# Batch 0 of a fused attention, gated-MLP and GLU kernel in another order, with its high parts on ScalarE, and w_out2's loads put behind batch 3's last weight piece

## The chip, the cores and the metric

One core of one Trainium2 chip runs the whole program. The metric is device time in microseconds (us). One run's profiled execution gives the trace; the times of other runs have no profile.

Five engines run their own instruction streams and wait for each other through semaphores: TensorE (PE, with its weight loads as PEld), VectorE (DVE), ScalarE (ACT), GpSimd (POOL) and SyncE (SP), which here only starts DMA transfers. Each engine works in order: an instruction that waits holds back everything behind it on its engine.

## The reference, cut to what matters

```python
# q, k, v: (4 batches, 8 heads, 576, 64)
scores = q @ k.T / 8 - slope[h] * |i - j|, kept where 0 <= i - j < 128
attn   = softmax(scores)
x      = concat_heads(attn @ v)                      # (4, 576, 512)
h      = gelu_tanh(x @ w_in)                         # w_in (512, 1024)
u, v   = h[..., :512], h[..., 512:]
vn     = (v - mean(v)) / sqrt(var(v) + 1e-6) * g_ln
vs     = w_sg @ vn + b_sg                            # mixes the 576 positions
x2     = x + (u * vs) @ w_out                        # (4, 576, 512)
h2     = relu(x2 @ w_in2)                            # w_in2 (512, 1024)
conv   = three-tap convolution of h2 over positions, per channel
out    = (h2 * sigmoid(conv)) @ w_out2               # w_out2 (1024, 512)
```

All inputs lie in DRAM; w_in, w_out, w_in2, w_out2 and the convolution's taps are 64-bit floats, read as pairs of 32-bit words.

## The kernel before, in words

**Precision.** Each large matrix product is made of three products of 32-bit "r" tiles: high by high, high by low, low by high. So each operand needs a high part (`copy` into a rounded tile, L188) and a low part (`tt`, the operand minus its high part, L200). `split` (L217) makes both. A 64-bit weight is first narrowed to 32 bits (`narrowed`, L268): a magnitude (L279 on ACT or L281 on DVE), a clamp (L283) and three bit operations on DVE (L284 to L286). The dictionary `ON` names which engines may take each kind of high and low part; `pick` (L177) takes the one with the least booked time.

**Phases.** STEPS holds three strings of steps, run in order. A step is a letter and indices. The first string is batch 0's attention in lower-case letters, then, woven together, batch b's MLP (capital V, U, G, W) and batch b+1's attention (capital L, M, C, E, N, T, A). The second is batch 3's MLP, the third the GLU (D and F). Names used below:

- `k` (L718) loads the position tables, the identity for transposes and g_ln, b_sg.
- `l m.half`, `v m.half` load q, k and v of head pair m (0 to 3); half 0 is rows 0 to 255, half 1 rows 256 to 575. The tag "st" has four buffers.
- `c` scores (PE `sc`, then masked by DVE into `t`, L530), `e` exponentials on ACT, `n` the division by the row sums (DVE `r`, then `scaled`, L215), `t` transposes (PE `pT`, evicted into `ph`), `z` the product with v (PE `o`, evicted into `x`).
- `X b.m.half` splits x into `xh`, `xl`.
- `j half.k` loads a piece of w_in, `i half.k` narrows and splits it into `win`. Half 1 is v's columns (four pieces, each one k-slice); half 0 is u's (four pieces, each one block m of 128 columns).
- `V b.j` (L608): v's product for rows block j (PE `psv`, 12 matmuls), gelu on ACT, mean and variance on DVE, then vn's high and low part. It needs all four pieces `i1.*`.
- `U b.half.m` (L638): u's product for column block m (PE `psu`, 12 matmuls), gelu. U0.0.m needs piece `i0.m`.
- `G` (PE `pss`, then L691 on DVE), `W` (PE `pso`, then x2 written to DRAM).
- `g` prepares w_sg (`prep32`), `o` w_out, `a i.c` a piece of w_in2 or w_out2: loaded, narrowed, split. Pieces prepared before the GLU's buffers exist are written to DRAM (`w2d`); the last twelve of w_in2 (LATE) go straight into their place.
- `w i.k.n` (L751) loads from DRAM what was prepared: w_in2's first part (i = 0, `w`) and w_out2 (i = 1, `wout`, eight transfers of 512 KB). Its instructions keep their place in the program.
- `x`, `y` load and split x2 for the GLU; D is the GLU's first product (PE `psg` from `x2g`), F its second (PE `psg` from `wout`).

A scheduler of the framework turns the list into one order for each engine by its own model of time; instructions under `keep_in_program_order` keep their place in the list. One tag "g" of two PSUM banks serves psv, psu, pss, pso in turn: a third product waits until the first is evicted.

The second string, where w_out2's loads stand:

```python
s = weave(n[:-6], put_by[LATE:]) + n[-6:]
for k in range(4):
    for h in range(2):
        s.insert(s.index("W3.0.0") + 3 * (2 * k + h), f"w1.{k}.{h}")
```

`n` is batch 3's MLP (29 steps), and `put_by[LATE:]` the last twelve pieces of w_in2.

## Time and profile before

| what | value |
|---|---|
| median of 3 runs | 599.72 us (599.45 to 600.98) |
| the profiled execution | 601.56 us, of which the trace's span is 599.8 us |
| granted TensorE clock, mean | 0.971 of full |
| busy PE / PEld | 561.9 / 483.6 us |
| busy DVE / ACT / POOL | 380.0 / 241.0 / 297.5 us |

Busy time counts instructions on an engine, not waiting. The chain of waits goes back from the last instruction to whatever released it; what an engine idles off that chain costs nothing. The profiled execution is 1.84 us above the median of the runs.

### The profile page before, as it was taken

Reading aid. Unit: us, or ns where it says so; the run is one execution under the profiler, and the core shown is the slowest. Engines: PE = TensorE matmul, PEld = TensorE weight load, DVE = VectorE, ACT = ScalarE, POOL = GpSimd, SP = SyncE. Lnnn points to the kernel's source line nnn. Section 1 sums busy time; section 2 is a strip of 40 time slices with the busy share of each in tenths; the row PEclk is TensorE's granted clock in tenths of the full one; section 3 lists DMA queues with packets and bytes.
Section 4 is the critical chain, followed back from the end, with each engine's and each line's share of the span. In section 5 each row is a group of like instructions: output and inputs, shape, how many; then the busy total and the mean of one; then the engine's idle time right before and its main releaser. Section 6 shows DMA issues by size and latency. Waiting matters only on the chain.

```text
span 599.8 us, 10377 instructions
## 1 busy us (share of the span) xinstructions
PE 561.9 (94%) x3744; PEld 483.6 (81%) x3744; DVE 380.0 (63%) x957; ACT 241.0 (40%) x610; POOL 297.5 (50%) x456
## 2 busy tenths in 40 slices
PE   6897499999999999999999899799799999999998
PEld 5564477879889798789798798799698889898887
DVE  4783658784485995795985787566865554545400
ACT  5484125863024743118732111244454434433401
POOL 2757512993142652344652543529877455545500
PEclk8896799899999999999999999899999999999999
DMA  8852014242225254241335335360210300100011
GB/s 283 280 186 81 23 40 146 87 130 62 84 75 146 60 166 148 87 145 37 119 104 158 105 107 152 130 209 1 74 43 19 114 19 19 55 19 19 17 54 53
DMA packets 44083, 57.78 MB, mean 96 GB/s; under 512 B 4096, under 2 KB 28672, under 8 KB 44032
## 3 DMA queue, kind: packets, MB, share of 16 engines
q1 hardware_dynamic: 43888, 56.99, 30.4%
q8 instruction: 29, 0.48, 0.3%
q14 instruction: 22, 0.18, 0.1%
q10 hardware_dynamic: 144, 0.13, 0.1%
HBM read 42.43 MB, written 14.68 MB: 95 GB/s over the span
## 4 chain that ended last, share of the span: by engine, by line
PE 64%; DVE 16%; POOL 8%; ACT 5%; DMA 3%; issue 2%; SPq 1%; POOLq 0%; ACTq 0%; DVEq 0%
PE psg L186 28%; PE psv L186 7%; PE pso L186 7%; PE psu L186 6%; PE sc L186 5%; PE o L186 5%; PE pss L186 3%; PE pT L446 2%; ACT t L160 2%; POOL t L215 2%; DVE wa L285 2%; DMA w<-in_w_in_dram 2%; DVE t L215 1%; DVE wa L283 1%; DVE wa L284 1%
## 5 line engine op out<-in xcount | busy, mean ns | idle before, releaser
L186 PE MATMUL psg<-x2g,w 128*128 128x288 f32 x768 | 108.0, 299 | 1.6 <-DVE x2g L204 1.2
L186 PEld LDWEIGHTS psg<-x2g,w 128*128 128x128 f32 x768 | 105.8, 191 | 3.9 <-DVE x2g L204 2.0
L186 PE MATMUL psg<-wout,gh 128*128 128x512 f32 (+1 forms) x272 | 81.3, 384 | 1.8 <-ACT gh L195 1.8
L160 ACT ACTIVATE t<-t,st 128x256 f32<-128x256 f32 (+2 forms) x144 | 67.2, 469 | 16.3 <-DVE st L530 9.9
L215 POOL TENSOR_SCALAR t<-t,r 128x256 f32<-128x256 f32 (+2 forms) x109 | 59.1, 558 | 19.5 <-DVE r L545 13.0
L186 PE MATMUL pss<-wsg,vn 128*128 128x256 f32 (+1 forms) x448 | 65.8, 304 | 2.7 <-DVE t L691 2.7
L186 PE MATMUL psu<-xh,win 128*128 128x256 f32 (+1 forms) x256 | 54.8, 308 | 11.1 <-POOL win L198 6.7
L186 PEld LDWEIGHTS pss<-wsg,vn 128*128 128x128 f32 x448 | 61.7, 195 | 4.1 <-DVE t L691 3.5
L817 DVE SCALAR_TENSOR_TENSOR cc<-hb,cw,cc 128x576 f32<-128x576 f32 x32 | 28.6, 893 | 50.0 <-POOL cc L215 50.0
L186 PE MATMUL pso<-gh,wo 128*128 128x256 f32 (+1 forms) x256 | 55.3, 308 | 5.0 <-DVE t L691 4.4
L186 PEld LDWEIGHTS psg<-wout,gh 128*128 128x128 f32 x272 | 49.5, 189 | 12.1 <-ACT gh L195 2.4
L186 PEld LDWEIGHTS psu<-xh,win 128*128 128x128 f32 x256 | 43.1, 198 | 13.6 <-POOL win L198 6.9
L186 PE MATMUL psv<-win,xh 128*128 128x512 f32 (+1 forms) x160 | 52.0, 403 | 1.8 <-POOL win L198 1.8
L186 PE MATMUL psg<-wout,gl 128*128 128x512 f32 (+1 forms) x136 | 52.2, 385 | 0.1
L215 POOL TENSOR_SCALAR cc<-hb,cw 128x576 f32<-128x576 f32 x32 | 27.6, 864 | 46.1 <-ACT hb L813 46.0
L186 PEld LDWEIGHTS pso<-gh,wo 128*128 128x128 f32 x256 | 41.1, 190 | 7.7 <-DVE t L691 4.8
L204 POOL TENSOR_TENSOR gl<-gg,gh 128x512 fp32r<-128x512 f32 x32 | 46.6, 1458 | 1.3 <-ACT gh L195 1.3
L204 POOL TENSOR_TENSOR t<-t,u 128x256 f32<-128x256 f32 (+1 forms) x32 | 27.7, 870 | 37.6 <-DVE t L691 28.9
L186 PE MATMUL sc<-k,q 64*128 64x256 f32 (+2 forms) x288 | 43.1, 372 | 0.2 <-DMA q<-in_q_dram 0.2
L813 ACT ACTIVATE hb<-psg 128x576 f32<-128x576 f32 x32 | 20.8, 652 | 55.7 <-PE psg L186 54.0
L186 PE MATMUL o<-ph,V 128*64 128x128 f32 (+2 forms) x448 | 41.1, 308 | 1.9 <-ACT ph L195 1.7
L204 DVE TENSOR_TENSOR gg<-cc,hb 128x576 f32<-128x576 f32 x32 | 30.3, 953 | 17.7 <-ACT cc L160 17.3
(87 smaller groups left out, 1069.9 us busy)
## 6 DMA issues: line engine op xcount, KB each, us to landing
w<-in_w_out_dram SPq DMA_DIRECT2D x24, 256.0 KB, 3.1
x2s<-x2d SPq DMA_DIRECT2D x16, 288.0 KB, 3.0
w<-in_w_in_dram SPq DMA_DIRECT2D x8, 512.0 KB, 5.6
w<-in_w_in_dram SPq DMA_DIRECT2D x16, 256.0 KB, 2.8
wout<-w2d SPq DMA_DIRECT2D x8, 512.0 KB, 4.4
V<-in_v_dram SPq DMA_DIRECT2D x12, 320.0 KB, 3.3
out_dram<-ot SPq DMA_DIRECT2D x15, 256.0 KB, 2.0
k<-in_k_dram SPq DMA_DIRECT2D x12, 288.0 KB, 3.2
```

What stands on the lines that cost most here:

```text
L160: ins = nc.scalar.activation(*args, **kw)
L186: return nc.tensor.matmul(out, lhsT, rhs, start=start, stop=stop, **kw)
L204: return (nc.vector if eng == "dve" else nc.gpsimd).tensor_tensor(dst, a, b, op=op)
L215: e.tensor_scalar(dst, src, col, 1.0, op0=ALU.mult, op1=ALU.mult)
L283: tc.keep_in_program_order(clamp.tensor_scalar(f(a), f(a), W_LOW, W_HIGH, op0=ALU.max, op1=ALU.min))
L284: nc.vector.tensor_scalar(a, a, 0x07FFFFFF, 3, op0=ALU.bitwise_and, op1=ALU.logical_shift_left)
L285: nc.vector.scalar_tensor_tensor(a, high, 0xC0000000, a, op0=ALU.bitwise_and, op1=ALU.bitwise_or)
L446: nc.tensor.transpose(ps[:, n * P : (n + 1) * P], s["t"][:, c0 : c0 + P], ident)
L813: nc.scalar.activation(h[:, 1 : S + 1].rearrange("p (a n) -> p a n", a=2), ps[:, :, :288], AF.Relu)
L817: nc.vector.scalar_tensor_tensor(cc, h[:, 0:S], cw[:, 0, c : c + 1], cc, op0=ALU.mult, op1=ALU.add)
```

## The change

In batch 0's list the steps stand in another order: V0.0 and V0.1 are parted, i0.2 stands before U0.0.0 and i0.3 before U0.0.2, and the second-half loads of pair 1 stand early, in buffers of another tag (w64). The tables are loaded per head pair in four transfers, not in two. The engines of batch 0's parts are fixed: the high parts of w_in, of x and of vn on ScalarE; the low parts of w_in and of x's first half on GpSimd; the divisions of the odd head (but for its last block) on VectorE and the others on GpSimd; the even head's evictions of first-half transposes on VectorE. The magnitude of six of w_in's eight pieces is on ScalarE. `prep32` (w_sg) keeps its high part's place in the list. In the second string w_out2's eight loads stand among the last six steps, behind the last piece of w_in2.

```diff
--- before.py
+++ after.py
@@ -35,9 +35,9 @@
 SLACK = 6000.0
 
 ON = {
-    "clamp": "dve", "w64 hi": "pool", "w64 lo": "pool", "w32 hi": "act pool", "w32 lo": "dve",
+    "clamp": "dve", "win hi": "act", "win lo": "pool", "w64 hi": "pool", "w64 lo": "pool", "w32 hi": "act pool", "w32 lo": "dve",
     "norm": "dve pool",
-    "x hi": "act pool", "x lo": "dve", "vn hi": "pool", "vn lo": "dve",
+    "x hi": "act pool", "x lo": "dve", "x first hi": "act", "x first lo": "pool", "x late hi": "act", "x late lo": "dve", "vn first hi": "act", "vn first lo": "dve", "vn hi": "pool", "vn lo": "dve",
     "gate": "pool", "g hi": "act dve pool", "g lo": "dve pool", "x2 hi": "act pool", "x2 lo": "dve",
     "tap": "act pool", "glu": "dve", "a hi": "act", "a lo": "pool",
     "edge hi": "pool", "edge lo": "pool",
@@ -73,10 +73,11 @@
     ]
     put_by = [f"a{i}.{c}" for i in (1, 0) for c in range(16)]
     s = """
-        k0 l0.0 k2 l1.0 k1 v0.0 l2.0 v1.0 l3.0 v2.0 v3.0 j1.0 j1.1 c0.0 e0.0 c1.0 n0.0 e1.0 i1.0 c2.0 e2.0 t0.0 n1.0 c3.0
-        e3.0 z0.0 X0.0.0 l0.1 v0.1 c0.1 e0.1 n2.0 t1.0 z1.0 X0.1.0 j1.2 j1.3 i1.1 n3.0 l1.1 v1.1 t2.0 z2.0 c1.1 e1.1 n0.1 i1.2
-        t3.0 z3.0 X0.2.0 X0.3.0 i1.3 j0.0 l2.1 c2.1 e2.1 n1.1 j0.1 t0.1 z0.1 j0.2 j0.3 i0.0 l3.1 v2.1 c3.1 e3.1 V0.0 V0.1 n2.1
-        t1.1 z1.1 i0.1 U0.0.0 X0.0.1 i0.2 n3.1 t2.1 v3.1 z2.1 X0.1.1 U0.0.1 i0.3 t3.1 z3.1 U0.0.2 U0.0.3 X0.2.1 X0.3.1 k3
+        k0 l0.0 k1 l1.0 k5 k2 l2.0 v0.0 k3 l3.0 v1.0 j1.0 v2.0 v3.0 j1.1 l1.1
+        c0.0 e0.0 c1.0 e1.0 l0.1 n0.0 j1.2 v0.1 c2.0 e2.0 t0.0 n1.0 c3.0 e3.0 l2.1 j1.3 v1.1 i1.0 z0.0 X0.0.0 t1.0 n2.0 z1.0 X0.1.0
+        i1.1 t2.0 n3.0 z2.0 X0.2.0 c0.1 e0.1 l3.1 j0.0 i1.2 t3.0 z3.0 X0.3.0 c1.1 e1.1 i1.3 n0.1 c2.1 e2.1 j0.1 j0.2 t0.1 n1.1 z0.1
+        v2.1 i0.0 c3.1 e3.1 j0.3 V0.0 t1.1 n2.1 z1.1 v3.1 i0.1 V0.1 t2.1 n3.1 z2.1 i0.2 U0.0.0 t3.1 z3.1 X0.0.1 U0.0.1
+        X0.1.1 i0.3 U0.0.2 X0.2.1 X0.3.1 U0.0.3 k4
     """.split()
     for b in range(B - 1):
         p = NP * (b + 1)
@@ -109,9 +110,8 @@
     n[n.index("W3.1.0")] += " y0.2"
     n[n.index("W3.1.1")] += " y0.3"
     s = weave(n[:-6], put_by[LATE:]) + n[-6:]
-    for k in range(4):
-        for h in range(2):
-            s.insert(s.index("W3.0.0") + 3 * (2 * k + h), f"w1.{k}.{h}")
+    late = [f"w1.{k}.{h}" for k in range(4) for h in range(2)]
+    s = s[:-6] + weave(s[-6:], late)
     second = " ".join(["x0.0.1.2.3"] + s)
     return first, second
 
@@ -265,7 +265,7 @@
 
     STAGE = dict(st=S, vn=1024, w64=512)
 
-    def narrowed(src, n, pool, tag, bufs, spool, stag, sbufs, act_abs=True):
+    def narrowed(src, n, pool, tag, bufs, spool, stag, sbufs, act_abs=False):
 
         if spool is None:
             st = src
@@ -275,7 +275,7 @@
         words = st[:, : 2 * n].rearrange("p (n w) -> p n w", w=2)
         low, high = words[:, :, 0], words[:, :, 1]
         a = pool.tile([P, 256 if tag == "wa" else 512], U32, tag=tag, name="wa", bufs=bufs)[:, :n]
-        if stag == "vn" and act_abs and pick(dict(act=52 + 0.85 * n, dve=67 + 0.52 * n)) == "act":
+        if act_abs:
             tc.keep_in_program_order(nc.scalar.activation(f(a), f(high), AF.Abs))
         else:
             tc.keep_in_program_order(nc.vector.tensor_scalar(a, high, 0x7FFFFFFF, None, op0=ALU.bitwise_and))
@@ -294,7 +294,8 @@
     def prep32(hi, lo, src, n, pool, tag, bufs):
         st = pool.tile([P, S], F32, tag=tag, name="wst", bufs=bufs)
         nc.sync.dma_start(st[:, :n], src)
-        split(hi, lo, st[:, :n], "w32")
+        tc.keep_in_program_order(copy(hi, st[:, :n], engines=ON["w32 hi"]))
+        tt(lo, st[:, :n], f(hi), ALU.subtract, ON["w32 lo"])
 
     def cols(w, k, c0, n):
 
@@ -311,12 +312,12 @@
             nc.sync.dma_start(st.rearrange("p (k n) -> p k n", k=NK), cols(w_in, slice(0, NK), k * P, P))
 
     def w_in_piece(half, k):
-        a = narrowed(w64.pop((half, k)), HF, mpool, "u", 4, None, "vn", 5, half == 1)
+        a = narrowed(w64.pop((half, k)), HF, mpool, "u", 4, None, "vn", 5, half == 1 or k < 2)
         if half:
-            split(winh[:, k, HF:], winl[:, k, HF:], a, "w64")
+            split(winh[:, k, HF:], winl[:, k, HF:], a, "win")
         else:
             sl = slice(k * P, (k + 1) * P)
-            split(winh[:, :, sl], winl[:, :, sl], a.rearrange("p (k n) -> p k n", k=NK), "w64")
+            split(winh[:, :, sl], winl[:, :, sl], a.rearrange("p (k n) -> p k n", k=NK), "win")
 
     def w_sg_piece(c):
         if c == 0:
@@ -479,14 +480,15 @@
         s = st8.setdefault((0, m), {})
         if half == 0:
             kq = apool.tile([P, 512], F32, tag="st", name="kq", bufs=NST)
-            s["k"], s["q"] = kq[:, :256], kq[:, 256:]
-            (nc.scalar if m == 0 else nc.sync).dma_start(s["q"], qT[0, m, :, :256])
-            nc.sync.dma_start(s["k"], kT[0, m, :, :256])
-        else:
-            s["k"] = apool.tile([P, 448], F32, tag="st", name="k", bufs=NST)
-            s["q"] = apool.tile([P, 320], F32, tag="st", name="q", bufs=NST)
-            nc.sync.dma_start(s["k"], kT[0, m, :, 128:])
-            nc.sync.dma_start(s["q"], qT[0, m, :, 256:])
+            s["k", half], s["q", half] = kq[:, :256], kq[:, 256:]
+            (nc.scalar if m == 0 else nc.sync).dma_start(s["q", half], qT[0, m, :, :256])
+            nc.sync.dma_start(s["k", half], kT[0, m, :, :256])
+        else:
+            tag, bufs = ("w64", 2) if m == 1 else ("st", NST)
+            s["k", half] = apool.tile([P, 448], F32, tag=tag, name="k", bufs=bufs)
+            s["q", half] = apool.tile([P, 320], F32, tag=tag, name="q", bufs=bufs)
+            nc.sync.dma_start(s["k", half], kT[0, m, :, 128:])
+            nc.sync.dma_start(s["q", half], qT[0, m, :, 256:])
 
     def z_vload(m, half):
         if half == 0:
@@ -521,7 +523,7 @@
             if of not in banks:
                 banks[of] = aps.tile([P, 512], F32, tag="a", name="sc", bufs=NA)
             d = slice(j * D, (j + 1) * D)
-            q, k = s["q"][d, q0 - 256 * half :][:, :nq], s["k"][d, k0 - 128 * half :][:, :nk]
+            q, k = s["q", half][d, q0 - 256 * half :][:, :nq], s["k", half][d, k0 - 128 * half :][:, :nk]
             mm(banks[of][d if i == 4 else slice(0, P), o : o + nk], q, k, start=True, stop=True)
         for j, i in z_blocks(half):
             o, nk = BLK[i][6], BLK[i][3]
@@ -546,7 +548,7 @@
         book("dve", 170)
         for j, i in z_blocks(half):
             e, c, _ = z_weights(m, half, j, i)
-            scaled(e, e, r[:, c - a : c - a + 1], ON["norm"])
+            scaled(e, e, r[:, c - a : c - a + 1], "dve" if j and i < 4 else "pool")
 
     def z_transpose(m, half):
         s = st8[0, m]
@@ -567,7 +569,7 @@
                 load["pe"] += 110
                 nc.tensor.transpose(ps[:, n * P : (n + 1) * P], src, ident)
             n = len(srcs) * P
-            copy(ph[:, :n], ps[:, :n], True)
+            copy(ph[:, :n], ps[:, :n], True, "act" if half or j else "dve")
             s["ph", half, j] = ph
 
     def z_av(m, half):
@@ -597,7 +599,7 @@
         x = xs[b, m][:, HALF[half]]
         hi = mpool.tile([P, n], F32R, tag=f"xg{half}", name="xh", bufs=8)
         lo = mpool.tile([P, n], F32R, tag=f"xg{half}", name="xl", bufs=8)
-        split(hi, lo, x, "x")
+        split(hi, lo, x, "x" if b else "x late" if half else "x first")
         xg[b, m, half] = (hi, lo)
 
 
@@ -632,7 +634,7 @@
         nc.gpsimd.tensor_scalar(rs[:r], ba[:r, 1:2], 1.0, 1e-6, op0=ALU.mult, op1=ALU.add)
         nc.gpsimd.tensor_tensor(rs[:r], rs[:r], mhalf[:r], op=ALU.pow)
         nc.vector.tensor_scalar(v[:r], v[:r], ba[:r, 0:1], rs[:r], op0=ALU.subtract, op1=ALU.mult)
-        split(hi[:r], lo if j < 4 else hi[64:], v[:r], "vn")
+        split(hi[:r], lo if j < 4 else hi[64:], v[:r], "vn" if b else "vn first")
         vns[b, j] = (hi, lo)
 
     def m_u(b, half, m):
@@ -716,11 +718,9 @@
 
 
     def constants(i):
-        if i == 0:
-            nc.sync.dma_start(tab[:, :1], tables[:, :1])
-        elif i == 1:
-            nc.sync.dma_start(tab[:, 1:], tables[:, 1:])
-        elif i == 2:
+        if i < NP:
+            nc.sync.dma_start(tab[:, i : i + 1], tables[:, i : i + 1])
+        elif i > NP:
             nc.sync.dma_start(ident, ident_c)
         else:
             nc.sync.dma_start(gln, g_ln)
```

## Rows read from the trace of the kernel before

**Rows 1.** Stages: window, length, each engine's busy us (instructions), granted clock, DMA

```profile
0.00:100.00 100.00, 80.89 (x511) 57.69 (x511) 61.92 (x208) 44.53 (x127) 48.52 (x80) 0.86 0.46 146
160.00:320.00 160.00, 158.59 (x1193) 135.46 (x1190) 126.15 (x407) 70.55 (x221) 73.37 (x130) 1.00 0.36 108
320.00:440.00 120.00, 109.37 (x708) 100.85 (x707) 85.38 (x156) 35.91 (x64) 64.17 (x90) 0.99 0.38 117
```

**Rows 2.** TensorE in order of time, 40 to 72 us (start, length, idle before)

```profile
50.90 1.22 PE L186 MATMUL psv<-win,xh 128*128 128x512 f32 x2 [0.33 <-POOL win L198]
...
69.87 0.58 PE L186 MATMUL psu<-xh,win 128*128 128x256 f32 x1 [6.72 <-POOL win L198]
```

**Rows 3.** GpSimd in order of time, 44 to 57 us

```profile
44.55 5.28 POOL L215 TENSOR_SCALAR t<-t,r 128x256 f32<-128x256 f32 x5 [0.85 <-DVE r L545]
49.81 1.04 POOL L198 TENSOR_SCALAR win<-wa 128x512 fp32r<-128x512 f32 x1
50.83 2.23 POOL L215 TENSOR_SCALAR t<-t,r 128x256 f32<-128x256 f32 x5
```

**Rows 4.** A slice of batch 0, columns as in the first group

```profile
50.00:60.00 10.00, 8.65 (x58) 5.70 (x58) 0.86 (x2) 4.41 (x9) 6.15 (x9) 0.69 0.23 64
```

**Rows 5.** VectorE in order of time, 50 to 71 us

```profile
57.82 0.49 DVE L204 TENSOR_TENSOR xl<-x,xh 128x320 fp32r<-128x320 f32 x1 [7.45 <-ACT xh L195]
...
69.38 0.98 DVE L286 SCALAR_TENSOR_TENSOR wa<-w,wa 128x512 uint32<-128x512 uint32 x1
```

**Rows 6.** psu's instructions alone, at the full and at the low clock

```profile
60.00:63.20 3.20, 3.13 (x24) 2.92 (x24) 0.39 (x1) 1.00 0.35 102
71.50:76.60 5.10, 5.07 (x23) 4.98 (x23) 0.38 (x1) 0.50 0.00 0
```

**Rows 7.** GpSimd's costliest groups, 0 to 77 us (busy us, mean ns, idle)

```profile
L215 POOL TENSOR_SCALAR t<-t,r 128x256 f32<-128x256 f32 x24 | 15.1, 642 | 3.9 <-ACT wa L279 1.9 <-DVE r L545 1.9
...
L198 POOL TENSOR_SCALAR win<-wa 128x512 fp32r<-128x512 f32 x8 | 6.2, 770 | 6.6 <-DVE wa L286 6.6
L215 POOL TENSOR_SCALAR t<-t,r 128x128 f32<-128x128 f32 x8 | 3.9, 492 | 11.1 <-DVE r L545 11.1
```

**Rows 8.** VectorE's divisions, one form, 160 to 240 us

```profile
L215 DVE TENSOR_SCALAR t<-t,r 128x256 f32<-128x256 f32 x12 | 5.3, 497 | 0.1
```

**Rows 9.** VectorE's groups, 0 to 77 us

```profile
L204 DVE TENSOR_TENSOR xl<-x,xh 128x256 fp32r<-128x256 f32 (+1 forms) x8 | 4.4, 547 | 8.8 <-ACT xh L195 7.5 <-POOL xh L198 1.4
...
L204 DVE TENSOR_TENSOR wsg<-wst,wsg 128x576 fp32r<-128x576 f32 x3 | 2.4, 806 | 0.0
L281 DVE TENSOR_SCALAR wa<-w 128x512 uint32<-128x512 uint32 x5 | 2.0, 404 | 0.9 <-DMA w<-in_w_in_dram 0.9
...
L197 DVE COPY ph<-pT 128x384 f32<-128x384 f32 x1 | 0.5, 545 | 0.0
```

**Rows 10.** ScalarE's groups, 0 to 77 us

```profile
L279 ACT ACTIVATE wa<-w 128x512 f32<-128x512 f32 x3 | 2.0, 683 | 0.0
...
L195 ACT CAST xh<-x 128x320 fp32r<-128x320 f32 x4 | 1.9, 466 | 0.0
```

**Rows 11.** Chain of waits, 374 to 384 us (start, us, what)

```profile
374.83 6.35 DMA w<-in_w_in_dram
```

**Rows 12.** VectorE in order of time, 376 to 383 us

```profile
381.20 0.29 DVE L281 TENSOR_SCALAR wa<-w 128x256 uint32<-128x256 uint32 x1 [4.24 <-DMA w<-in_w_in_dram]
```

**Rows 13.** TensorE in order of time, 378 to 385 us

```profile
383.13 0.56 PE L186 MATMUL pso<-gh,wo 128*128 128x320 f32 x2 [3.62 <-DVE t L691]
```

**Rows 14.** SyncE's issues, 372 to 377 us

```profile
372.97 0.32 SPq L761 DMA_DIRECT2D wout<-w2d  x1
```

**Rows 15.** Page, DMA issues: count, KB each, median us to landing

```profile
w<-in_w_in_dram SPq DMA_DIRECT2D x16, 256.0 KB, 2.8
```

**Rows 16.** psg's instructions alone, before and behind that wait

```profile
366.60:368.40 1.80, 1.74 (x12) 1.61 (x12) 0.00 (x0) 1.00 0.63 148
384.70:387.50 2.80, 2.73 (x12) 2.75 (x12) 0.00 (x0) 0.53 0.00 0
```

## The prediction

> **What bounds the kernel now.** I first read the table by stage. From 160 to 320 us TensorE is busy 158.6 of 160 us at the full clock; from 0 to 100 us only 80.9, at 0.86 of the clock, and from 320 to 440 us 109.4 of 120 [rows 1]. So time can be had at two places, which the change touches, and between them TensorE passes on a shift one for one.
>
> Then I read TensorE's order in batch 0. Its last psu columns wait 6.72 us, to 69.87 us, for GpSimd's high part of a w_in piece, and before that the fourth k-slice of psv starts at 50.90, as another high part ends [rows 2]. GpSimd's order shows why: from 44.55 us on it works without a pause, five divisions, a high part, five divisions, more parts [rows 3]. What should be seen: the first five divisions take 5.28 us and the next five 2.23 us. They are the same work; the second five ran while VectorE, 0.86 us busy in that slice, stood still [rows 4]. VectorE waits 7.45 us there, to 57.82, for `xh`, which hangs on those divisions through the transposes; its last step on a w_in piece ends only at 70.36 us [rows 5]. The price is paid again in the clock: 24 psu matmuls take 3.13 us at the full clock, and behind the wait 23 take 5.07 us at half of it [rows 6].
>
> **Batch 0, part by part.**
>
> *GpSimd.* It loses the divisions of j = 1 but for its last block (16: 12 by 642 ns and 4 by 492 ns, 9.7 us), eight high parts of win (6.2 us) [rows 7] and the four high parts of x's first half. It gains four low parts of 256 columns; the trace has no such x, and I bound one by a win high part above (770 ns) and by half of it below, 1.5 to 3.1 us. The trace's 9.7 and 6.2 less 1.5 to 3.1 make some 13 to 14 us less, in an engine that paces 44 to 57 us. In that stretch two of each five divisions go (5.28 by 2/5 is 2.11, 2.23 by 2/5 is 0.89), and two high parts, the one shown with 1.04 us and one at the mean of 0.77 (sum 1.81) [rows 3, 7]. That is 4.8 us earlier for psv's last slice, for the transposes behind the divisions and so for `xh`.
>
> *VectorE.* It gains those 16 divisions, at most 497 ns each, 8.0 us [rows 8], and three more evictions of 545 ns, 1.6 us. It loses four low parts of x (2.2 us), three magnitudes (1.2 us) and, since w_sg's high part keeps its place behind the batch, three w_sg low parts (2.4 us) [rows 9]. Net +3.8 us. What hides it: the 7.45 us for which it waited [rows 5]. Without that cover it costs 3.8 us, and I keep that for the range. The three w_sg pieces come back behind U0.0.3, with u's and v's later blocks queued behind them on ScalarE and VectorE and pss waiting for the last; VectorE is busy 61.9 of the first 100 us [rows 1], so I take 0, and 2.4 us if there is no room.
>
> *ScalarE.* It gains eight high parts of 512 columns and three magnitudes, which I price alike, by the magnitude of that width: 11 by 683 ns, 7.5 us; and four xh at no more than 466 ns, 1.9 us [rows 10]. It is 4.4 us busy in the ten from 50 to 60 us [rows 4], so half of it fits where it waited; the rest falls among the exponentials before 45 us. I take 0 on the path, with 9.4 us as the other end.
>
> *Order.* The piece i0.2 stands before U0.0.0 rather than behind X0.0.1, so its VectorE work can fill the 7.45 us; i0.3 stands no earlier against t3.1 than it did. I give this nothing beyond covering VectorE's 3.8 us. Where psu then doesn't stand still for 6.72 us, the clock holds: 24 matmuls at the rate of 5.07 us for 23 are 5.3 us, against 3.13, so 2.2 us come back [rows 6]. The tables in four transfers and pair 1's loads in w64 change arrivals by a few tenths of a microsecond; 0. The high parts of vn change engine at about the same price; 0.
>
> Sum for batch 0: 4.8 + 2.2 = 7.0 us. Low end: no gain and 9.4 us of ScalarE's work in series, so 9.4 lost. High end: the whole wait of 6.7 us besides, 13.7 gained.
>
> *A rule against the change.* The rows show that a division on GpSimd takes 1.06 us beside a full VectorE and 0.45 us beside an idle one [rows 3, 4]. The Trainium skill ("GPSIMD Engine Reference", section 8, Key points) says that GpSimd shares its SBUF interfaces with VectorE and contends with those of VectorE's instructions that run in a two-port mode or have two SBUF inputs. Read strictly, divisions split over both engines hardly run side by side, and only the high parts (1.8 us) would come off the 44 to 57 us stretch, not 4.8; the sum would be 3.0 us less, 591.2 us. No row has a division on both at once, so I keep the row's arithmetic and count this among the rivals.
>
> **w_out2's loads.** The chain of waits holds a 256 KB load of w_in2, issued at 374.83 us, for 6.35 us [rows 11]. VectorE stands 4.24 us before its first instruction on it [rows 12], and queued behind it is L691's eviction of pss, which frees the PSUM bank that pso needs: TensorE waits 3.62 us [rows 13]. A 512 KB load of w_out2 went out at 372.97 on the same queue [rows 14]. The median of such w_in2 loads is 2.8 us [rows 15]. With 2.8 the piece lands 3.55 us sooner, and L691 follows on at once, so of the 3.62 us about 3.5 go. The clock falls in that wait: 12 psg take 2.73 us behind it and 1.74 before [rows 16], 1.0 us back. Sum 4.5 us; if the load is slow anyway, 0. On SyncE's queue the eight loads move past the last w_in2 pieces and stand with batch 3's x2 writes; the GLU's later x2 loads stay behind them. What hides them is the GLU's first columns, which run before psg first reads `wout`, so I charge 0; were the last 512 KB one late, it would cost what is left of one transfer, and the longest that I have a row for is the 6.35 us of rows 11.
>
> **Sum.** 7.0 + 4.5 = 11.5 us off the profiled execution's 601.56 (span 599.8 and 1.76 around it), that is 590.1. The median of the runs lies 1.84 lower, so 588.2; I say 588.
>
> **The rivals.**
>
> 1. *ScalarE paces batch 0, slower.* For: it carries the exponentials, waits in order, and a high part stuck behind a block of them holds psv or psu as GpSimd's did. Against: it has 4.4 of 10 us busy where the wait is [rows 4]. If its 9.4 us come in series and w_out2's 4.5 us are gained: 599.7 + 9.4 - 4.5 = 604.6. It decides against the change once more than 4.5 of the 9.4 us are on the path. Chance 0.13.
> 2. *The two engines stretch each other.* Divisions split over GpSimd and VectorE take as long as on one, and GpSimd's stretch shrinks by 1.8 rather than 4.8 us: 588.2 + 3.0 = 591.2. For: rows 3 themselves; against: GpSimd's list is much shorter. Chance 0.12, which is that of the page's rule too. *VectorE's added 3.8 us show:* 592.0. Chance 0.08.
> 3. *Only one of the two halves works.* w_out2's wait is replaced (DVE waits for another piece, or the bank is late for another reason): 588.2 + 4.5 = 592.7. Or batch 0 gives nothing and w_out2 does: 588.2 + 7.0 = 595.2. Chance 0.15.
> 4. *Nothing measurable.* Batch 0 loses what the end gains: 598 to 601.5. Chance 0.07.
> 5. *More.* The last psu loses its whole wait: 588.2 - 6.7 = 581.5. For: VectorE is idle there [rows 5]. Chance 0.15.
> 6. My forecast, 586 to 591: 0.3.
>
> **How the numbers follow.** A measurement of this kernel tells about 0.3%, 1.8 us, from no change: 597.9 to 601.5 counts as the same. Cases 2, 3, 5 and 6 are faster, 0.8; case 4 the same, 0.07; case 1 slower, 0.13. The range leaves out most of case 1 and little at the low end: 578 (case 5 with half of the 7.45 us of VectorE's wait besides) to 600.
>
> **What would show it.** In batch 0: no high part of win on GpSimd, and its chain before psv's last slice gone; the last psu ends near 70 us where it was 76.6; psu's wait under 3 us, with the full clock; VectorE's wait of 7.45 us gone. At the end: the w_in2 load near 375 us (then near 368) lands in about 3 us, no wait of TensorE for L691 over 1 us, and a granted clock of 1.0 where it was 0.53 [rows 16]. I am wrong if ScalarE's or VectorE's queue holds psv as long as GpSimd's did, or if pss waits longer near 100 us because the w_sg pieces come late.

## The result and the profile after

The kernel after runs in 595.10 us (median of 19 runs), the kernel before, timed beside it, in 601.27 us (19 runs). The ratio is 0.9907, with a 95% interval of 0.9886 to 0.9928: 5.6 us faster by the ratio, where 11.5 us were forecast. The profiled execution took 596.58 us (span 594.7, mean clock 0.980), so in the traces the change is worth 5.1 us of span.

The table by stage of the kernel after, columns as in [rows 1]:

```profile
0.00:100.00 100.00, 81.87 (x554) 61.21 (x554) 72.35 (x230) 58.32 (x173) 38.80 (x60) 0.91 0.48 152
50.00:60.00 10.00, 6.41 (x64) 5.19 (x64) 8.99 (x19) 7.85 (x18) 6.21 (x6) 0.94 0.32 93
60.00:70.00 10.00, 8.60 (x40) 7.55 (x39) 3.73 (x5) 1.17 (x3) 2.80 (x3) 0.72 0.00 0
160.00:320.00 160.00, 158.61 (x1188) 135.83 (x1187) 125.46 (x405) 72.00 (x222) 73.09 (x129) 1.00 0.37 110
320.00:440.00 120.00, 111.81 (x734) 103.13 (x733) 89.52 (x159) 37.11 (x66) 69.27 (x97) 1.00 0.35 114
```

Between 50 and 60 us VectorE is now 8.99 us busy, against 0.86 [rows 4], and ScalarE 7.85 against 4.41: the work has moved where it was meant to. From 320 to 440 us TensorE is busy 2.4 us longer in the same stretch than in [rows 1]. TensorE's order in batch 0, and then psu's instructions from 59.4 us on alone:

```profile
59.45 1.46 PE L186 MATMUL psu<-xh,win 128*128 128x256 f32 x3 [2.97 <-ACT win L195]
...
66.71 0.38 PE L186 MATMUL psu<-xh,win 128*128 128x256 f32 x1 [1.31 <-ACT win L195]
...
70.87 0.28 PE L186 MATMUL psu<-xl,win 128*128 128x256 f32 x1
...
74.65 2.72 PE L186 MATMUL sc<-k,q 64*64 64x192 f32 x20
```

```profile
59.40:65.20 5.80, 5.67 (x24) 5.27 (x24) 0.00 (x0) 0.50 0.00 0
```

The last psu ends at 71.2 us, not 76.6 [rows 6], and the longest wait for a high part is 2.97 us, not 6.72 [rows 2]. ScalarE, not GpSimd, is now what TensorE waits for. But the 24 psu behind the 2.97 us still run at half the clock, 5.67 us, as 23 did in 5.07 [rows 6]. GpSimd and then VectorE in order of time:

```profile
47.23 1.64 POOL L215 TENSOR_SCALAR t<-t,r 128x256 f32<-128x256 f32 x3 [4.09 <-ACT xh L195]
50.06 1.27 POOL L204 TENSOR_TENSOR win<-wa,win 128x512 fp32r<-128x512 f32 x1 [1.19 <-ACT win L195]
...
57.03 4.48 POOL L204 TENSOR_TENSOR win<-wa,win 128x512 fp32r<-128x512 f32 x2 [3.45 <-ACT win L195]
```

```profile
47.52 1.07 DVE L215 TENSOR_SCALAR t<-t,r 128x256 f32<-128x256 f32 x2
...
50.30 1.31 DVE L281 TENSOR_SCALAR wa<-w 128x512 uint32<-128x512 uint32 x1
...
60.31 1.48 DVE L281 TENSOR_SCALAR wa<-w 128x512 uint32<-128x512 uint32 x1 [1.16 <-POOL win L204]
...
63.48 0.69 DVE L286 SCALAR_TENSOR_TENSOR wa<-w,wa 128x512 uint32<-128x512 uint32 x1
72.16 0.70 DVE L631 BATCH_NORM_STATS2 bs<-v 128x6 f32<-128x512 f32 x1 [7.98 <-ACT v L160]
```

GpSimd has no high part of win and stands still between its pieces. VectorE's wait of 7.45 us [rows 5] is gone. Its last step on a w_in piece ends at 64.17 us, where it ended at 70.36 us, and the wait that is left, 7.98 us, comes after all that work.

So far it goes as forecast: the first scores of batch 1, which stand behind one more product of V0 (two before), start at 74.65 us, where they started at 82.35 us before. That is 7.7 us; the forecast for batch 0 was 7.0. But the first product of V1.0, the beginning of batch 1's MLP, starts at 152.26 us, before at 153.65 us. The two lines, after and before:

```profile
152.26 0.62 PE L186 MATMUL psv<-win,xh 128*128 128x512 f32 x2
...
153.65 0.63 PE L186 MATMUL psv<-win,xh 128*128 128x512 f32 x2
```

Of the 7.7 us 6.3 are lost in between. SyncE's issues in that stretch, GpSimd's first high parts of w_sg, the chain of waits, and TensorE's two longest waits:

```profile
34.07 0.33 SPq L296 DMA_DIRECT2D wst<-in_w_sg_dram  x1
...
42.38 0.43 SPq L296 DMA_DIRECT2D wst<-in_w_sg_dram  x1
...
77.40 0.35 SPq L296 DMA_DIRECT2D wst<-in_w_sg_dram  x1
...
80.95 0.33 SPq L363 DMA_DIRECT2D q<-in_q_dram  x1
81.63 5.41 SPq L296 DMA_DIRECT2D wst<-in_w_sg_dram  x2
87.38 0.33 SPq L274 DMA_DIRECT2D w<-in_w_out_dram  x1
87.81 0.37 SPq L363 DMA_DIRECT2D k<-in_k_dram  x1
...
112.89 0.33 SPq L363 DMA_DIRECT2D q<-in_q_dram  x1
```

```profile
77.65 1.48 POOL L198 TENSOR_SCALAR wsg<-wst 128x576 fp32r<-128x576 f32 x2
```

```profile
87.38 3.22 DMA w<-in_w_out_dram
...
91.61 2.85 DMA w<-in_w_out_dram
...
112.89 2.84 DMA q<-in_q_dram
115.87 4.22 PE sc L186 x20
```

```profile
102.50 1.28 PE L447 MATMUL pT<-ident,t 128*128 128x128 f32 x4 [3.08 <-POOL t L215]
...
115.87 4.22 PE L186 MATMUL sc<-k,q 64*64 64x192 f32 x20 [2.50 <-DMA q<-in_q_dram]
```

Two loads of w_sg leave at 34 and 42 us into buffers of the tag "st". Their pinned high parts run only from 77.65 us, and the low parts, which read the buffers last, end at 80.9 and 81.6 us: until then two of the four buffers are taken. The third load, at 77.40 us, gets a buffer that batch 1's first scores have just read; a `q` at 80.95 and the fourth load at 81.63 us get those of w_sg. `w_out`'s and batch 1's loads queue behind them. The pieces of `w_out` are staged in the same buffers, and the `q` of 112.89 us leaves as VectorE has read one of them. So TensorE waits 3.08 us before 102.50 us for a division on GpSimd and 2.50 us at 116 us for that `q`, and then computes scores for 4.22 us that take 2.72 us at 74.65.

At the end the shift from V3.0's start on is 3.7 us. SyncE's issues there, the loads from 360 to 380 us, and TensorE's waits behind 310 us (us in total, times, longest):

```profile
373.18 0.82 SPq L274 DMA_DIRECT2D w<-in_w_in_dram  x2
374.04 0.90 SPq L761 DMA_DIRECT2D wout<-w2d  x2
```

```profile
w<-in_w_in_dram SPq DMA_DIRECT2D x4, 256.0 KB, 3.0
```

```profile
PE psg L186 <- POOL gl L204: 2.7, 3, 1.1
...
PE pso L186 <- DVE t L693: 0.7, 1, 0.7
```

The w_in2 loads land in 3.0 us (6.35 in [rows 11]) and the wait of 3.62 us [rows 13] is down to 0.7. From 380 to 390 us TensorE is busy 9.97 of 10 us at a clock of 1.00. In its place psg waits 2.7 us for GpSimd's low parts `gl` in the GLU, a wait that the kernel before doesn't have; psg's waits in all grow from 3.3 to 4.5 us.

### The profile page after: what moved, and what is told of

The parts are those of the page before. It is cut to its first block, busy times and chain, and to the rows that moved or that the text cites. A ratio compares the mean times of both kernels' runs of the same rounds, so it can differ in the third digit from the quotient of the medians.

```text
span 594.7 us, 10374 instructions
## 1 busy us (share of the span) xinstructions
PE 558.2 (94%) x3744; PEld 481.2 (81%) x3744; DVE 387.8 (65%) x962; ACT 248.5 (42%) x626; POOL 286.9 (48%) x435
## 4 chain that ended last, share of the span: by engine, by line
PE 67%; DVE 15%; ACT 6%; POOL 6%; DMA 3%; issue 2%; SPq 1%; ACTq 0%; POOLq 0%; DVEq 0%
PE psg L186 29%; PE pso L186 7%; PE psv L186 7%; PE psu L186 6%; PE pss L186 5%; PE sc L186 5%; PE o L186 5%; PE pT L447 3%; ACT t L160 3%; DVE t L215 2%; POOL gl L204 1%; DVE wa L285 1%; POOL cc L215 1%; DMA w<-in_w_out_dram 1%; DVE wa L281 1%
## 5 line engine op out<-in xcount | busy, mean ns | idle before, releaser
L186 PE MATMUL psg<-x2g,w 128*128 128x288 f32 x768 | 106.6, 296 | 0.5 <-ACT x2g L195 0.3
L186 PEld LDWEIGHTS psg<-x2g,w 128*128 128x128 f32 x768 | 104.5, 188 | 2.7 <-DVE x2g L204 0.7
L215 POOL TENSOR_SCALAR t<-t,r 128x256 f32<-128x256 f32 (+2 forms) x95 | 49.1, 533 | 28.6 <-DVE r L547 11.3
L817 DVE SCALAR_TENSOR_TENSOR cc<-hb,cw,cc 128x576 f32<-128x576 f32 x32 | 27.0, 848 | 48.3 <-POOL cc L215 48.3
L215 POOL TENSOR_SCALAR cc<-hb,cw 128x576 f32<-128x576 f32 x32 | 29.3, 917 | 46.8 <-ACT hb L813 46.8
L204 DVE TENSOR_TENSOR gg<-cc,hb 128x576 f32<-128x576 f32 x32 | 33.5, 1053 | 17.6 <-ACT cc L160 17.6
L186 PEld LDWEIGHTS o<-ph,V 128*64 128x64 f32 x448 | 26.7, 139 | 18.4 <-ACT ph L195 5.4
```

The costliest lines, as they stand in the source:

```text
L186: return nc.tensor.matmul(out, lhsT, rhs, start=start, stop=stop, **kw)
L204: return (nc.vector if eng == "dve" else nc.gpsimd).tensor_tensor(dst, a, b, op=op)
L215: e.tensor_scalar(dst, src, col, 1.0, op0=ALU.mult, op1=ALU.mult)
L817: nc.vector.scalar_tensor_tensor(cc, h[:, 0:S], cw[:, 0, c : c + 1], cc, op0=ALU.mult, op1=ALU.add)
```

## The experiments

Each ratio is the median against that of the kernel before on the same chip, with its 95% interval. The places in the table are starts in TensorE's order of time, from one profile of each kernel: batch 1's first scores, V1.0, V3.0, and the span. A is from the scores to V1.0, B from V3.0 to the end. The last column is the longest wait of pso for pss's eviction near 383 us [rows 13], and the granted clock of the 4 us behind it where it fell.

| kernel | ratio | scores | V1.0 | V3.0 | span | A | B | pso's wait |
|---|---|---|---|---|---|---|---|---|
| before | 1 | 82.35 | 153.65 | 323.21 | 599.8 | 71.3 | 276.6 | 3.62, 0.58 |
| after | 0.9907 | 74.65 | 152.26 | 321.81 | 594.7 | 77.6 | 272.9 | 0.7 |
| e1: after, w_sg free | 0.9875 | 75.91 | 149.30 | 318.84 | 592.7 | 73.4 | 273.9 | 0.7 |
| e2: after, w_out2 as before | 0.9913 | 75.25 | 152.92 | 322.48 | 597.1 | 77.7 | 274.6 | 3.00 |
| e3: before + w_out2 late | 0.9979 | 84.50 | 155.83 | 325.37 | 599.2 | 71.3 | 273.8 | 0.7 |
| e4: before + w_sg pinned | 1.0115 | 81.39 | 163.35 | 333.01 | 609.1 | 82.0 | 276.1 | 2.65, 0.57 |
| e6: before + engines | 0.9983 | 81.31 | 155.19 | 324.73 | 601.4 | 73.9 | 276.7 | 3.37, 0.57 |
| e7: before + order | 0.9891 | 78.60 | 149.89 | 319.43 | 593.2 | 71.3 | 273.8 | 2.09 |
| e8: e1 + edges on ScalarE | 0.9810 | 75.39 | 148.82 | 318.38 | 590.9 | 73.4 | 272.5 | 0.7 |
| e9: e7 + w_out2 late | 0.9881 | 77.89 | 149.17 | 318.72 | 592.7 | 71.3 | 274.0 | 0.7 |
| e10: e9 + edges on ScalarE | 0.9862 | 77.03 | 148.36 | 317.92 | 591.1 | 71.3 | 273.2 | 0.7 |
| e11: before + loads | 0.9958 | 82.77 | 154.11 | 323.65 | 598.0 | 71.3 | 274.4 | 2.80 |
| e12: before + edges on ScalarE | 0.9983 | 82.76 | 154.19 | 323.76 | 600.4 | 71.4 | 276.6 | 3.31, 0.60 |
| e13: e8 + w_out behind G0 | 0.9980 | 73.92 | 155.09 | 324.63 | 598.0 | 81.2 | 273.4 | 0.7 |

Kernels with the same batch 0 (before, e3, e12) differ by up to 2.2 us at the scores, so a place in one profile tells nothing finer than that. A is steadier: 71.3 to 71.4 in seven kernels. A profile is one execution, and the executions of one kernel differ in their clock: those of the kernel after run from 593.38 us at a mean clock of 0.990 to 600.82 us at 0.969. The profiled one lies 2.2 to 3.0 us above its kernel's median in e2, e4, e6 and e8, and 1.0 us under it in e10. So the ratios say what a kernel is worth, and the spans only where time lies.

**e1, the change with w_sg's pieces free.**

```diff
-        tc.keep_in_program_order(copy(hi, st[:, :n], engines=ON["w32 hi"]))
-        tt(lo, st[:, :n], f(hi), ALU.subtract, ON["w32 lo"])
+        split(hi, lo, st[:, :n], "w32")
```

> The changed kernel, but w_sg's high part is free to move again (prep32 as before the change). Theory A: the changed kernel is 7.7 us ahead of the old one at batch 1's first scores and 1.4 us ahead at V1.0, and gives the 6.3 us between back because the high part that keeps its place holds two of the four st buffers from 34 to 77 us, so that q of later pairs lands late. Then here the lead at V1.0 is 5 us or more, TensorE's 3.7 us of waits for q are under 1 us, and the kernel is 4 to 6 us faster than the changed one, about 0.983 of before. Theory B: batch 1's attention on ScalarE, VectorE and GpSimd bounds 84 to 125 us in any case, and TensorE only arrives sooner. Then the lead at V1.0 stays at 1 to 2 us and the time stays at 0.99 of before.

Measured: 0.9875 [0.9842, 0.9907]. SyncE sends w_sg's third load at 42.6 us with the second, batch 1's next `k` and `q` follow at 47.7 and 48.7 us, and the waits for `q` and for the division are gone:

```profile
42.61 0.80 SPq L296 DMA_DIRECT2D wst<-in_w_sg_dram  x2
47.67 0.33 SPq L362 DMA_DIRECT2D k<-in_k_dram  x1
48.68 0.33 SPq L362 DMA_DIRECT2D q<-in_q_dram  x1
```

A falls from 77.6 to 73.4 us and V1.0 comes 3.0 us sooner, a lead of 4.4 us where theory A asked for 5 or more; the ratio falls short of its 0.983. The interval overlaps that of the change itself, so the time alone would not settle it; e4 does.

**e4, the reverse: the pinned high part alone, in the kernel before** (e1's diff the other way round).

> The kernel before with only w_sg's high part held at its place. Theory A: batch 0 gets lighter by up to 2.4 us of VectorE's work, but q of batch 1's later pairs lands late and 3 to 6 us are lost between 92 and 154 us; 2 to 5 us slower in all, 1.003 to 1.008 of before, with waits of TensorE for q of 2 us or more. Theory B: no loss there; 0.996 to 1.0 of before.

Measured: 1.0115 [1.0078, 1.0151], slower by 6.9 us; A is 82.0 us. TensorE's waits to 160 us show what comes late:

```profile
PE psu L186 <- POOL win L198: 7.0, 1, 7.0
PE pso L186 <- POOL gl L204: 5.7, 2, 5.5
...
PE sc L186 <- DMA q<-in_q_dram: 2.8, 1, 2.8
```

The psu wait was there before [rows 2]; the `q` wait and the late `gl` are the pin's. So the pin costs: by the times in the old list, by A in the new one. Giving w_sg's pieces staging buffers of their own was not tried.

**e2, the change with w_out2's loads where they were.**

```diff
-    late = [f"w1.{k}.{h}" for k in range(4) for h in range(2)]
-    s = s[:-6] + weave(s[-6:], late)
+    for k in range(4):
+        for h in range(2):
+            s.insert(s.index("W3.0.0") + 3 * (2 * k + h), f"w1.{k}.{h}")
```

> The changed kernel with w_out2's eight loads where they were. If their move gained what the prediction said, TensorE waits 3 us or more for the eviction of pss again near 375 us, the lead at the end of the span falls from 5 to 1 or 2 us, and the time is 0.996 to 1.0 of before. Rival: the wait went away because batch 0 runs otherwise and shifts the pieces; then the time stays at 0.99 and there is no such wait.

Measured: 0.9913 [0.9881, 0.9945]. The wait of pso for pss's eviction is back (3.7 us, longest 3.0) and `gl` no longer holds psg, so B is 1.7 us longer in the profile. But the clock held behind the wait, and by the times the move can't be told from nothing here. Neither forecast holds whole: the wait is back, and the time stays at 0.99.

**e3, w_out2's move alone in the kernel before** (e2's diff the other way round).

> The kernel before with only w_out2's loads moved. Prediction's term: 4.5 us faster, 0.9925 of before, no wait of TensorE over 1 us for the eviction near 380 us, the w_in2 load there landing in about 3 us. Rival: the wait is only moved on to another piece or to the GLU's first columns; within 0.3% of before.

Measured: 0.9979 [0.9956, 1.0002]. TensorE's waits behind 310 us:

```profile
PE psg L185 <- POOL gl L203: 2.2, 2, 1.4
...
PE pso L185 <- DVE t L690: 0.7, 1, 0.7
```

The move does what it says to the wait, 0.7 us where it was 3.62. B is 2.8 us shorter, although psg's waits in the GLU grow from 3.3 to 4.5 us, 2.2 of them for `gl`; the times have 1.3 us, between 2.6 and none, which is the rival's case and not the prediction's 4.5.

**e6, the engines alone in batch 0's old list** (the hunks of `ON`, `narrowed`, `w_in_piece`, `scaled`, `copy(ph...)`, `x` and `vn`).

```diff
+    "win hi": "act", "win lo": "pool", ...
+            scaled(e, e, r[:, c - a : c - a + 1], "dve" if j and i < 4 else "pool")
...
```

> The kernel before with only the engines of batch 0's parts changed (high parts on ScalarE, divisions split, low parts of x's first half on GpSimd); the list, the loads, w_sg and w_out2 as before. The prediction put batch 0's 7 us on GpSimd's shorter queue and nothing on the order: then psu's wait of 6.7 us shrinks, batch 1's first scores start 5 to 8 us sooner than at 82.4 us, and the kernel is 0.985 to 0.993 of before. Rival: without the new order the added ScalarE and VectorE work holds psv and psu as long as GpSimd did; first scores at 80 us or later, 0.995 to 1.005.

Measured: 0.9983 [0.9954, 1.0013]: nothing. GpSimd's high parts are gone, and psu now waits for its low parts:

```profile
PE psu L186 <- POOL win L204: 4.5, 2, 3.7
...
PE psu L186 <- ACT win L195: 2.4, 2, 1.4
PE psv L186 <- POOL win L204: 2.0, 2, 1.3
```

**e7, the list, the early loads and the tables alone**, engines, w_sg and w_out2 as before.

```diff
-        ... V0.0 V0.1 n2.1 t1.1 z1.1 i0.1 U0.0.0 X0.0.1 i0.2 ...
+        ... V0.0 t1.1 n2.1 z1.1 v3.1 i0.1 V0.1 t2.1 n3.1 z2.1 i0.2 U0.0.0 ...
+            tag, bufs = ("w64", 2) if m == 1 else ("st", NST)
...
```

> The kernel before with only batch 0's list, its loads and tables changed; engines, w_sg and w_out2 as before. Prediction: the order gives nothing by itself; first scores of batch 1 within 2 us of 82.4 us, 0.995 to 1.005 of before, GpSimd still holding psv and psu. Rival: the order is what counts; first scores 4 us sooner or more, 0.985 to 0.993.

Measured: 0.9891 [0.9854, 0.9928], as much as the whole change. In the profile 3.8 us of it are there at V1.0, and 2.8 us come in B, which the order doesn't touch (e11 has the same). Its slice from 50 to 60 us, to hold against [rows 4], and TensorE's longest wait for a piece:

```profile
50.00:60.00 10.00, 8.54 (x64) 6.57 (x58) 6.45 (x14) 5.66 (x14) 9.67 (x13) 0.83 0.35 95
```

```profile
PE psu L187 <- POOL win L199: 3.5, 1, 3.5
```

GpSimd is as full as one can be, 9.67 of 10 us, with all its divisions and high parts. VectorE is 6.45 us busy where it was 0.86, since the pieces' narrowing stands in the list where it used to wait, and its last step on a piece ends at 67.34 us, not at 70.36 [rows 5]. Which of the list's moves does it was not taken apart further than e11 does.

**e11, of these the tables and the early loads alone.**

```diff
-        k0 l0.0 k2 l1.0 k1 v0.0 l2.0 ... j1.1 c0.0 ... n3.0 l1.1 v1.1 ...
+        k0 l0.0 k1 l1.0 k5 k2 v0.0 l2.0 ... j1.1 l1.1 c0.0 ... n3.0 v1.1 ...
+            tag, bufs = ("w64", 2) if m == 1 else ("st", NST)
```

> The kernel before with only the tables in four transfers and pair 1's second-half loads early, in the w64 buffers; the rest of the list as before. Prediction: a few tenths of a microsecond; first scores of batch 1 within 2 us of 82.4 us, 0.997 to 1.003 of before. Rival: the earlier arrivals carry the order's gain; 0.988 to 0.994.

Measured: 0.9958 [0.9934, 0.9983], 2.5 us. The scores don't move (82.77 us); the profile has it in B. TensorE's wait for pss's eviction and the 4 us behind it:

```profile
382.70 0.56 PE L186 MATMUL pso<-gh,wo 128*128 128x320 f32 x2 [2.80 <-DVE t L692]
```

```profile
384.00:388.00 4.00, 4.00 (x31) 4.00 (x31) 3.87 (x10) 1.43 (x3) 2.28 (x3) 1.00 0.00 0
```

In the kernel before the clock of those 4 us is 0.58, with 20 matmuls in them; here 31, at 1.00. The table's last column shows it of all: with w_out2's loads in their old place and the clock down, B is 276.1 to 276.7 us (before, e4, e6, e12); with the clock kept, 273.8 to 274.6 (e2, e7, e11). The line of the kernel before, for the same 4 us:

```profile
384.00:388.00 4.00, 4.00 (x20) 4.00 (x20) 3.85 (x8) 1.61 (x3) 2.10 (x3) 0.58 0.00 0
```

The two groups lie 2.2 us apart. Some 0.6 of that is the wait itself (3.2 us in the mean of the first, 2.6 of the second), so the clock's price is some 1.6 us of B. The wait's length alone doesn't tell whether the clock falls: it fell behind 2.65 us (e4) and not behind 3.00 (e2). Each row is one execution, and the clock differs between executions of one kernel, so the table doesn't show that the new list or the early loads keep the clock up. The times say that the loads are worth 1.0 to 4.0 us; that it is by this clock is argued. Why the same loads make TensorE wait 2.1 us in one kernel and 3.6 in another was not settled.

**e9 and e10, the order with w_out2's move, and then with the GLU's edge high parts on ScalarE too.** The edge parts are 64 of a column's 576 positions, split into high and low by themselves. e10's second edit is this line, and e8 and e12 make it as well:

```diff
-    "edge hi": "pool", "edge lo": "pool",
+    "edge hi": "act", "edge lo": "pool",
```

> The kernel before with the new list, loads and tables of batch 0 and with w_out2's loads moved; engines and w_sg as before. New theory: the order carries batch 0's gain and the engines give back between 84 and 153 us what they gain before it. Then this is as fast as the changed kernel with w_sg free, or faster: 0.983 to 0.988 of before, V1.0 at 149 to 151 us. Rival: the engines are worth 2 to 4 us beside the order; 0.990 to 0.993.

> The same with the GLU's edge high parts on ScalarE. If GpSimd holds the GLU's first columns and takes w_out2's gain, this is 1 to 3 us faster than without, 0.978 to 0.985 of before, with no wait of TensorE for GpSimd's low parts after 395 us. Rival: within 0.3% of the same kernel without it.

Measured: e9 0.9881 [0.9848, 0.9915], e10 0.9862 [0.9830, 0.9893]. In e9 psg waits 3.4 us for `gl`, in e10 that wait is gone, and psg's wait for ScalarE's `gh` grows from 1.1 to 2.0 us. The order's gain stands without any of the engines' part. The times tell neither w_out2's move beside it (e7 has 0.9891) nor the edge parts: e10 lies 0.2% under e9, inside the rival's 0.3%.

**e12, the edge parts alone in the kernel before.**

> The kernel before with only the GLU's edge high parts on ScalarE. If GpSimd's queue bounds the GLU's first columns in any kernel, 1 to 3 us faster, 0.995 to 0.998 of before. If it does so only once w_out2's wait is gone (the kernel before has no wait of TensorE for GpSimd's low parts there), within 0.3%.

Measured: 0.9983 [0.9958, 1.0007]. Where nothing waits for `gl`, moving these parts does nothing that the times can tell.

**e8, the change with w_sg free (e1) and the edge parts on ScalarE.**

> The changed kernel with w_sg's high part free, and the GLU's 64-column edge high parts on ScalarE, not GpSimd. Theory: in the moved kernels GpSimd is 10 of 10 us busy from 400 to 420 us and TensorE waits 2 to 3 us for its low parts, which is where the rest of w_out2's 4.5 us went; with 32 operations of some 0.7 us less on GpSimd those waits fall under 1 us and the time is 1 to 3 us under the kernel with w_sg free alone. Rival: the first GLU columns are a chain of latencies, not of GpSimd's load; no change beyond 0.3%.

Measured: 0.9810 [0.9776, 0.9845], 589.94 us, the fastest of all, 11.4 us under the kernel before by the ratio. B is 272.5 us, 1.4 shorter than e1's, with no wait for `gl` left. It beats both kernels. Against e10, which has all of it but the engines, the intervals overlap; against e1 they only touch.

**e13, e8 with the first halves of two w_out pieces behind the first gate products.** It asks why A is 73.4 us with the new engines and 71.3 without. In e8 VectorE is 3.9 to 4.9 of each 5 us busy from 75 to 100 us and pss waits 2.8 us for L692, which stands behind w_out's narrowing.

```diff
+            uv = weave(uv, ...)
+            s += [x for x in uv if x not in ("o2.0", "o3.0")] + ["o0.1"] + gw[:2] + ["o1.1"] + gw[2:4] + ["o2.0", "o2.1"] ...
```

> This is the version with w_sg's pieces free and the edge parts on ScalarE, with the first halves of two of w_out's four pieces (steps o2.0, o3.0) moved behind the first gate products. Theory: the lead that batch 0 gains melts between the first scores and V1.0 because VectorE's queue is full there (4.3 to 4.9 of each 5 us from 75 to 100 us), with w_out's narrowing ahead of L692's eviction of pss; about 4.8 us of that narrowing (two pieces of some 2.2 to 2.5 us) then go behind it. So pss's wait of 2.8 us falls under 1 us, the half clock behind it goes too, the stretch from the first scores to V1.0 falls from 73.4 to about 70 to 71 us, and the ratio from 0.981 to about 0.976. Rival: ScalarE sets it, 5.0 of 5 us busy from 95 us on with batch 1's exponentials, and VectorE's place is a coincidence: pss's wait goes but the stretch stays at 73 to 74 us, ratio 0.981. Second rival: W0's product then waits for w_out, in the place of the wait removed: a wait of pso over 1.5 us near 115 us, ratio 0.981 to 0.985.

Measured: 0.998 [0.9951, 1.0008], 1.7% slower than e8's ratio. The wait of pss is gone, as the theory said; the second rival then takes more than it gave, on another engine:

```profile
PE pso L187 <- POOL gl L205: 4.9, 1, 4.9
```

GpSimd works without a pause from 100 to 120 us in both kernels; with w_out's parts behind it, `gl` comes 4.9 us late, and the half clock follows (0.50 from 115 to 120 us). So VectorE's queue does hold pss in e8, and taking work out of its way there is no gain, since GpSimd's has no slack to take it.

## Why the prediction was right in direction and half in size

11.5 us were forecast, and the traces have 5.1. Two steps failed: batch 0's gain was given to GpSimd's shorter list, where the order makes it; and it was carried to the end whole, with w_sg's pinned high part at 0, where 6.3 us of it are lost between the first scores and V1.0. From V1.0 to V3.0 the lead does pass on one for one (169.56 us before, 169.55 after). A smaller part of the distance from 588 to 595.1 us, 1.6 us, lies in the base: the kernel before had a median of 599.72 us in 3 runs and of 601.27 in 19.

**GpSimd's list, 4.8 us, and "Order. ... I give this nothing".** This step failed in its mechanism. The sum for batch 0 came out at the right size at its own place, 7.7 against 7.0 us, but that is luck, for it did not come from the term that I gave it to: the engines alone (e6) are worth nothing that the times can tell, and the order, priced at nothing, brings 3.8 us by V1.0 alone (e7; 4.5 and 5.3 in e9 and e10, which have the same batch 0). I had read the wait of 6.72 us as GpSimd's queue being long. In e6, without GpSimd's high parts, psu still waits 4.5 us for its low parts. [Rows 5] held the other reading: VectorE's 7.45 us idle stood in the same stretch, and its work on the pieces came after it. Filling that wait moves the last pieces although GpSimd stays as full as before.

**psu's clock, 2.2 us.** Not returned: a shorter wait of 2.97 us still left 24 psu at 0.50, 5.67 us. In the sum for the scores' place the order made up for it.

**VectorE's 3.8 us, hidden.** Held: its last w_in step ends 6.2 us sooner with the added work.

**ScalarE's 9.4 us, 0 on the path.** Between the ends that I gave. psu waits 5.1 us for ScalarE's high parts in three pieces, rival 1's mechanism, but not so long as for GpSimd's before. With the engines the scores come about 2 us sooner than with the order alone (75.4 and 75.9 in e8 and e1, 77.0 to 78.6 in e7, e9 and e10), and A is 2.1 us longer (2.6 in e6): by V1.0 nothing is left. That the lead melts in queues without slack is shown for pss (e13), but pss waits 2.1 us in e10 too and 2.8 in e8, so this is not all. One cause I had overlooked: the edit names batch 0's parts only, but `pick` gives later parts to the engine with the least booked time, and with batch 0's parts off GpSimd it gives GpSimd more of batch 1. Between the first scores and V1.0 GpSimd has 24 divisions of 128x256 in e1, e8 and e6 and 21 in before, e7, e9 and e10; it also gets two high parts of w_sg and one or two low parts `gl` of 320 columns that it has in none of those four. It is busy 41.8 to 42.0 us there against 40.2 to 40.3, and from 100 to 130 us it doesn't pause in e8 nor, but for 0.1 us, in e10. That is close to the 2.1 us, but no run holds batch 1's engines fixed, so what share is GpSimd's and what VectorE's stays open.

**w_sg, 0, or 2.4 if there is no room.** This is the term that takes most of what is missing: priced at 0, it measures 4.2 us of A (1.9 by two ratios whose intervals overlap), and for another reason than I gave. I had counted the VectorE work that comes back and the place of pss. What costs is that the pieces' loads stay early while their copies are pinned late: two of four "st" buffers are held from 34 or 42 to 81 us, and SyncE, in order, holds w_sg's next loads, `w_out`, `k` and `q` behind them. In the old list it is 10.7 us of A and 1.15% of the time. With the 2.1 us above that is the 6.3.

**w_out2, 3.5 and 1.0 us.** The mechanism held to the row: the loads land in 3.0 us, TensorE's wait for that eviction (L691 before, L693 after) is 0.7 us and the clock 1.00. The sum did not: 4.5 us were forecast, B is 2.8 us shorter in e3, and the times there have 1.3 us. psg waits 2.2 to 3.4 us for `gl` in after, e1, e3 and e9, which I charged nothing: GpSimd's list in the GLU, 10.00 of 10 us busy from 400 to 410 us in the kernel after and 5.92 before, comes last next. e8 and e10 show it, where the edge parts leave GpSimd and that wait goes. And the clock's 1.0 us is some 1.6, but only where the clock falls; in the profiles with the new order it stays up without the move (e7, e2), and there the move brings 1.7 us of B (e2 to after) or none (e7 to e9).

**The rivals.** The sum of what happened is 7.7 gained, 6.3 given back, 3.7 gained at the end, 5.1 us. That lies nearest to rival 3 (one half only, 595.2 us), but not by its mechanism: both halves worked at their place, and each paid for a queue behind it. Rival 2 speaks of divisions on both engines. At 47 us GpSimd divides at 0.55 us each beside VectorE at 0.54, against 0.45 beside an idle VectorE [rows 3] and 0.50 in VectorE's mean [rows 8]; there they run side by side.

## What to carry to other kernels

Where one engine is late and another idles in the same stretch, try the order first: let the idle engine's work come before what it waits for, and only then move work between engines. A step that is held late must not keep its load early: the buffer that it holds delays every load behind it on the queue. Follow a lead to the next stages before it is counted, for here 7.7 us at one place were 1.4 us some 78 us later. Where a program shares out later work by booked time, look at what an edit of one stage does to the engines of the next.

## What the runs showed of the hardware that was not expected

A VectorE instruction with one input is stretched by a GpSimd subtraction. L281 on 128x512 took 0.40 us before [rows 9]; in the kernel after the two that run beside GpSimd's low parts of win took 1.31 and 1.48 us, and each ended 0.28 us after GpSimd did (51.33 and 51.61, 61.51 and 61.79). In e7 one took 1.40 us beside such a low part and ended 0.29 us after it. The Trainium skill ("GPSIMD Engine Reference", section 8, Key points) says that GpSimd contends with VectorE's instructions that run in a two-port mode or have two SBUF inputs. By that rule the stretched L281, which has one input, ran in a two-port mode, which no trace here shows; and VectorE's divisions, which have one input and a column, were hardly stretched beside GpSimd's (0.54 us). Beside a GpSimd product of two inputs one was: a division of 128x192 took 1.04 us in e8, from 119.61 us, and ended 0.13 us after the product. GpSimd's slow divisions of [rows 3] ran beside VectorE's instructions of which seven of the nine longest have two inputs, and there the trace agrees with the page.

A DMA wait in a later stage can come from a load some 70 us before: w_sg's loads of 34 and 42 us set when the `q` of 112.89 us could leave; with w_sg free (e1) TensorE has no such wait.
